# Two attention and two MLP layers on one core: the last 64 contraction rows of the projections as half-array pairs, with some reordering

## The chip, the core and the metric

The kernel runs on one core of one Trainium2 chip. The core has TensorE (PE: matrix multiplication into the accumulator memory, PSUM), VectorE (DVE), ScalarE (ACT), GpSimd (POOL) and SyncE (SP), which here issues the DMA transfers. Each engine works through its own instructions in order; the engines wait for each other by semaphores. The metric is the device time of one execution in microseconds (us), lower is better; the time before is the median of three runs.

## The reference

`x` has 2048 tokens of width 576. Four layers follow each other, A, B, A, B, each on the layer norm of `x` and added to it. The two A layers share their weights, and so do the two B layers.

```python
def _A_ref(x, wqkv, wo):
    B, S, D = x.shape
    H = 32; Dh = D // H                      # 18
    qkv = (x @ wqkv).reshape(B, S, 3, H, Dh).transpose(2, 0, 3, 1, 4)
    q, k, v = qkv[0], qkv[1], qkv[2]
    phi = lambda t: jnp.where(t > 0, t + 1, jnp.exp(t)) + 1e-6
    pq, pk = phi(q), phi(k)
    kv = jnp.einsum("bhsd,bhse->bhde", pk, v)
    z = jnp.einsum("bhsd->bhd", pk)
    num = jnp.einsum("bhqd,bhde->bhqe", pq, kv)
    den = jnp.einsum("bhqd,bhd->bhq", pq, z)[..., None] + 1e-6
    o = num / den
    return o.transpose(0, 2, 1, 3).reshape(B, S, D) @ wo

def _B_ref(x, w1, b1, w2, b2):               # D = 576, F = 4608
    y = _layernorm(x, axis=-1)
    h = _gelu(jnp.einsum("bsd,df->bsf", y, w1) + b1)
    return jnp.einsum("bsf,fd->bsd", h, w2) + b2

x = x + _A_ref(_layernorm(x), wqkv, wo)
x = x + _B_ref(_layernorm(x), w1, b1, w2, b2)
x = x + _A_ref(_layernorm(x), wqkv, wo)
x = x + _B_ref(_layernorm(x), w1, b1, w2, b2)
```

## The kernel before

The tokens are cut into 16 tiles of 128 (`NT`). The width 576 is the contraction of the projections; it is cut into five chunks (`KD`), four of 128 rows and one of 64. `yT` holds the normalised tokens transposed, chunk by chunk. In the fifth chunk only 64 of the 128 rows carry data in an A layer; the other 64 rows of the weights `wqkv_sb` are set to zero (L188), so the fifth matmul of every group runs on the full array with half of it at zero.

**Normalisation** (`LNPipe`, L234 to L350). `feed` enters a tile, each `tick` moves every entered tile one stage on: statistics on DVE (L266, L267, L272, L275), the root on POOL (L284), the normalisation on DVE (L303) or POOL (L288, L299), and the transposition into `yT`: by TensorE and a copy for the first six tiles of layer 0 (L324 to L332), by a DMA for all others (L343). In B layers POOL also copies the last 64 columns a second time beside themselves (L307), so that both halves of the fifth chunk carry them.

**Layer A** (`layer_A`, L399). A loop runs over the 16 tiles. In each, `k_proj` makes the keys in two halves of 288 columns, five matmuls each, in two buffers of the pool `ps_h` (four banks), followed by phi (`phi_from_psum`: two ACT passes, L361 and L363, and two DVE passes, L364 and L368). `v_proj` makes the values in two parts of 252 and 324 columns, five matmuls each, in the one buffer `accB` of the pool `ps_acc`; ACT copies 504 columns out (L438) and DVE the last 72 (L447). `kv_acc` of the tile before adds keys times values to `kvacc` (in `accA`), and from tile 4 on one block of `q_proj` (a group of heads `g`, a chunk of 512 tokens `c`) makes the queries, five matmuls of 512 columns. TensorE's order is exactly the order of the code (`pe` chains the instructions). In layer 0 `pre_a1` also feeds later tiles' normalisation; in layer 2 nearly all of that is done before.

After the loop come the masks of `kvacc` (L485), its product with `wo` (`kv_wo`, in `accB` and `accA` in turn, copied out by DVE or ACT, L512 and L514), the denominators (`den_stage`, `scale_stage`), the eight query blocks that are left, and the output stage: for each of 16 tiles `wo_stage` makes ten matmuls and `residual` adds the old rows on DVE into a buffer `xn` (L390, four buffers), which is stored and, for the first four tiles, normalised by POOL.

**Layer B** (`LayerB`). The first product of the MLP already runs as half-array pairs (L648): two matmuls of 64 contraction rows at once, one on each half of the array, in different PSUM banks. The second product (L695) uses the full array.

**Order.** Each engine's order is set when the program is built: a scheduler keeps the dependencies that `add_manual_dep` adds (`NOSYNC` ones only fix an order on an engine) and otherwise places instructions by readiness. SP's start-up DMAs follow the chain of `chained`: the first two token tiles, the keys' weights, a token tile, the values' weights, three token tiles, the queries' weights, the rest.

Of the kernel before, what the change touches and what calls it, by code (L numbers as in the profile page):

```python
# [17 lines left out]
KD = 5  # L18
# [16 lines left out]
def build(tc, A_x, A_wqkv, A_wo, B_w1, B_b1, B_w2, B_b2, out, dbg=None, n_layers=4):  # L35
    nc = tc.nc
    dbg = dbg or {}
    with ExitStack() as ctx:
# [71 lines left out]
        NV = 3  # L110
# [18 lines left out]
        x0_tiles = {}  # L129

# [30 lines left out]
        def load_wqkv(part):  # L161
            cols = slice(part * D, (part + 1) * D)
            chained(nc.sync.dma_start(out=wqkv_sb[:, 0:4, cols],
                                      in_=A_wqkv[0:4 * P, cols].rearrange("(k p) n -> p k n", p=P)))
            chained(nc.sync.dma_start(out=wqkv_sb[0:64, 4, cols], in_=A_wqkv[4 * P:D, cols]))
# [22 lines left out]
        nc.vector.memset(wqkv_sb[64:P, 4, :], 0.0)  # L188
        for vr in v_ring:
            nc.gpsimd.memset(vr[:, 4, 72:126], 0.0)  # L190
            nc.gpsimd.memset(vr[:, :, 126:127], 1.0)
            nc.gpsimd.memset(vr[:, :, 127:128], 0.0)

# [40 lines left out]
        class LNPipe:  # L234
# [3 lines left out]
            def feed(self, xt, t, kind, norm_eng, evac_eng="dve", load_from=None, after=None):  # L238
# [3 lines left out]
                                       after=after, xbar=xbar))  # L242
# [4 lines left out]
            def tick(self, transposes=1):  # L247
                for it in list(self.items):
# [14 lines left out]
                    elif st == 0:  # L263
# [8 lines left out]
                        nc.vector.bn_aggr(out=mv[:], in_=stt[:])  # L272
# [18 lines left out]
                    elif st in (2, 3):  # L291
# [10 lines left out]
                        else:  # L302
                            norm = nc.vector.tensor_scalar(out=y[:, 0:D], in0=xt[:, 0:D], scalar1=it["mv"][:, 0:1],  # L303
                                                           scalar2=it["rstd"][:, 0:1], op0=ALU.subtract, op1=ALU.mult)
                            dve_last["norm"] = norm.ins.name
                        if it["kind"] == "B":
# [12 lines left out]
                    elif st == 4:  # L319
                        y = it["y"]  # L320
                        t = it["t"]
                        tp = ps_h.tile([P, 8, P], BF16, name="tp", tag="h")
                        for k in range(KD):
                            pe(nc.tensor.transpose(out=tp[:, k, :], in_=y[:, k * P:(k + 1) * P], identity=ident[:]))  # L324
                        if it["evac"] == "both":
                            part = nc.vector.tensor_copy(out=yT[:, 0:2, t * P:(t + 1) * P], in_=tp[:, 0:2, :])  # L326
                            dve_last["turn"] = part.ins.name
                            nc.scalar.copy(out=yT[:, 2:KD, t * P:(t + 1) * P], in_=tp[:, 2:KD, :])
# [30 lines left out]
        def phi_from_psum(ps_ap, out_ap, rows, n, after=None):  # L359
            e = work.tile([P, 512], BF16, name="phi_e", bufs=3)  # L360
            act_last["exp"] = nc.scalar.activation(out=e[0:rows, 0:n], in_=ps_ap, func=ACT.Exp).ins.name  # L361
            a = work.tile([P, 512], BF16, name="phi_a", bufs=2)
            nc.scalar.activation(out=a[0:rows, 0:n], in_=ps_ap, func=ACT.Identity, bias=C1, scale=1.0)  # L363
# [21 lines left out]
        def residual(li, t, halves):  # L385
            xo = xo_of.pop((li, t))
            last = (li == n_layers - 1)
            xn = work.tile([P, D], F32, name="xn", tag="xn", bufs=4)
# [10 lines left out]
        def layer_A(li, next_kind, pre_a1=None, mid_k0=None):  # L399
            kvacc = ps_acc.tile([P, 2, 512], F32, name="kvacc", tag="accA")  # L400
# [4 lines left out]
            def k_proj(t, mid=None):  # L405
                tok = slice(t * P, (t + 1) * P)
                pk = blk.tile([P, D], BF16, name="pk", tag="blk")
                for half in range(2):
                    kp = ps_h.tile([P, 512], F32, name="k_ps", tag="h")
                    for k in range(KD):  # L410
                        pe(nc.tensor.matmul(kp[:, 0:HALF], lhsT=yT[:, k, tok],  # L411
                                         rhs=wqkv_sb[:, k, D + half * HALF: D + (half + 1) * HALF],
                                         start=(k == 0), stop=(k == KD - 1)))
# [6 lines left out]
            def v_proj(t):  # L420
# [6 lines left out]
                else:  # L427
                    vp = ps_acc.tile([P, 2, 512], F32, name="v_ps", tag="accB")
                    vps = None
                    first, second = vp[:, 0, :], vp[:, 1, :]  # L430
                for k in range(KD):
                    pe(nc.tensor.matmul(first[:, 0:252], lhsT=yT[:, k, tok], rhs=wqkv_sb[:, k, 2 * D: 2 * D + 252],  # L432
                                     start=(k == 0), stop=(k == KD - 1)))
                for k in range(KD):
                    pe(nc.tensor.matmul(second[:, 0:324], lhsT=yT[:, k, tok], rhs=wqkv_sb[:, k, 2 * D + 252: 3 * D],  # L435
                                     start=(k == 0), stop=(k == KD - 1)))
                if vps is None:
                    nc.scalar.copy(out=va[:, 0:4, 0:126].rearrange("p (b g) c -> p b g c", b=2),  # L438
                                   in_=vp[:, :, 0:252].rearrange("p b (g c) -> p b g c", g=2))
# [18 lines left out]
            def q_proj(g, c):  # L458
                qp = ps_h.tile([P, 512], F32, name="q_ps", tag="h")
                for k in range(KD):  # L460
                    pe(nc.tensor.matmul(qp[0:GR[g], :], lhsT=wqkv_sb[:, k, GO[g]:GO[g] + GR[g]],  # L461
                                     rhs=yT[:, k, c * CA:(c + 1) * CA],
                                     start=(k == 0), stop=(k == KD - 1)))
                pq[(g, c)] = blk.tile([P, D], BF16, name="pq", tag="blk")
                phi_from_psum(qp[0:GR[g], :], pq[(g, c)][0:GR[g], 0:CA], GR[g], CA)
# [3 lines left out]
            for t in range(NT):  # L469
# [9 lines left out]
                if t >= 4:  # L479
                    q_proj(*q_left.pop(0))  # L480
# [340 lines left out]
```

## Time and profile before

| | us |
|---|---|
| median of the runs (772.94, 774.46, 774.32) | 774.32 |
| profiled execution | 772.56 |
| its span, first to last instruction | 770.8 |
| TensorE busy | 760.2 |
| ACT, DVE, POOL busy | 329.0, 243.8, 124.9 |

The granted TensorE clock is 0.999 of full speed. By stages of the span:

| stretch, us | what runs | TensorE | DVE | ACT | POOL |
|---|---|---|---|---|---|
| 0 to 20 | layer 0, start and tiles 0 to 3 | 15.66 | 14.04 | 9.39 | 7.78 |
| 20 to 66.7 | layer 0, rest of the loop over tiles | 46.70 | 34.92 | 35.42 | 29.30 |
| 66.7 to 107.4 | layer 0, output stage | 39.40 | 34.09 | 23.68 | 10.12 |
| 107.4 to 389.2 | layer 1 (B) | 281.80 | 64.67 | 98.81 | 37.58 |
| 389.2 to 444.6 | layer 2, loop over tiles | 55.40 | 28.47 | 40.80 | 0.55 |
| 444.6 to 485.3 | layer 2, output stage | 39.40 | 34.09 | 23.63 | 10.07 |
| 485.3 to 770.8 | layer 3 (B) | 281.85 | 33.49 | 97.32 | 29.56 |

How to read the lines: a timeline line has the start in us, the time taken, the engine, the line of the code, the operation, what it writes and reads, the shapes and, after x, how many like it are merged. A bracket gives the idle time before it on its engine and what ended it. A line of the view by stretches has the bounds, the length and then the busy time of TensorE, of its weight loads, of DVE, ACT and POOL, the clock and the DMA share and rate. Matmuls overlap: the next one starts before the last has left the array, so what counts is the distance from start to start, not the duration that is shown.

### The profile page before, as it was taken

How to read it: one execution, taken by the hardware profiler on the slowest of the kernel's cores; microseconds unless marked ns; L12 is line 12 of the kernel's file. 1: busy time of each engine (PE TensorE's matmuls, PEld its weight loads, DVE VectorE, ACT ScalarE, POOL GpSimd, SP SyncE). 2: the span in 40 equal slices, each digit the busy share in tenths (PEclk: the TensorE clock that was granted, in tenths of full speed). 3: DMA queues.
4: the chain of work that ended last, by engine and by line, in shares of the span. 5: the costliest groups of instructions: out<-in, count | busy, mean ns of one | idle time of the engine just before them, and what ended most of it. 6: DMA issues, size and time to landing. Idle time of an engine off the chain costs nothing.

```text
span 770.8 us, 15615 instructions
## 1 busy us (share of the span) xinstructions
PE 760.2 (99%) x6516; PEld 490.0 (64%) x6520; DVE 243.8 (32%) x678; ACT 329.0 (43%) x733; POOL 124.9 (16%) x208
## 2 busy tenths in 40 slices
PE   7999999999999999999999999999999999999998
PEld 4776654675477457646777766547745764674476
DVE  7776952125013402301244488353000000000000
ACT  4777546304610650263057784460065026205600
POOL 3680412013000301100100004221010010011000
PEclk9999999999999999999999999999999999999999
DMA  8799484025112502400310038775100110011000
GB/s 257 160 242 327 129 275 97 19 62 131 45 40 73 143 2 64 94 2 24 89 47 1 1 108 263 201 147 89 46 26 1 32 62 1 13 43 39 2 29 18
DMA packets 77904, 66.41 MB, mean 86 GB/s; under 512 B 44682, under 2 KB 62474, under 8 KB 77834
## 3 DMA queue, kind: packets, MB, share of 16 engines
q1 hardware_dynamic: 77834, 65.42, 31.7%
q8 instruction: 51, 0.84, 0.5%
q14 instruction: 19, 0.16, 0.1%
HBM read 39.38 MB, written 16.52 MB: 73 GB/s over the span
## 4 chain that ended last, share of the span: by engine, by line
PE 92%; DVE 4%; POOL 2%; ACT 1%; issue 1%; POOLq 0%; DVEq 0%
PE m_ps L695 37%; PE h_ps L648 20%; PE hp_ps L648 16%; PE k_ps L411 5%; PE q_ps L461 5%; PE wo_ps L549 3%; PE v_ps L435 3%; PE v_ps L432 2%; PE kvacc L455 1%; DVE xn L390 1%; POOL ln_rstd L284 1%; POOL ln_nmr L288 1%; POOL y_ring L299 1%; DVE pq L541 0%; ACT rden_bc L540 0%
## 5 line engine op out<-in xcount | busy, mean ns | idle before, releaser
L695 PE MATMUL m_ps<-w_sb,hT 128*128 128x288 bf16 x2304 | 283.6, 286 | 0.0
L695 PEld LDWEIGHTS <-hT 128*128 128x128 bf16 x2304 | 224.8, 98 | 59.8 <-issue 3.4
L648 PEld LDWEIGHTS <-w_sb 64*128 64x128 bf16 x2304 | 124.5, 94 | 136.2 <-issue 1.9
L648 PE MATMUL hp_ps<-yT,w_sb 64*128 64x512 bf16 x1152 | 178.0, 376 | 0.0
L390 DVE TENSOR_TENSOR xn<-m_ps,x_ring 128x576 f32<-128x576 f32 (+1 forms) x32 | 24.2, 757 | 411.6 <-PE m_ps L695 411.6
L648 PE MATMUL h_ps<-yT,w_sb 64*128 64x512 bf16 x1152 | 147.9, 376 | 0.0
L653 ACT COPY relay_sb<-relay_sb 128x1 f32<-128x1 f32 x144 | 28.5, 198 | 265.7 <-PE h_ps L648 222.2
L644 ACT ACTIVATE hT<-h_ps,b1T 128x512 bf16<-128x512 f32 x144 | 91.0, 683 | 43.3 <-PE h_ps L648 43.3
L284 POOL TENSOR_TENSOR ln_rstd<-ln_u,neg_half 128x1 f32<-128x1 f32 x64 | 36.8, 576 | 359.7 <-DVE ln_u L275 229.5
L644 ACT ACTIVATE hT<-hp_ps,b1T 128x512 bf16<-128x512 f32 x144 | 91.1, 692 | 0.0
L382 POOL TENSOR_TENSOR x_ring<-x_ring,b_bc 128x576 f32<-128x576 f32 x32 | 40.7, 1275 | 240.6 <-DMA x_ring<-x_d 237.9
L648 PE MATMUL h_ps<-yT,w_tail 64*128 64x512 bf16 x144 | 54.1, 376 | 0.0
L648 PE MATMUL hp_ps<-yT,w_tail 64*128 64x512 bf16 x144 | 54.1, 376 | 0.0
L461 PE MATMUL q_ps<-yT,wqkv_sb 128*126 128x512 bf16 (+1 forms) x200 | 50.0, 382 | 0.1
L549 PE MATMUL wo_ps<-kvwo,pq 126*128 126x288 bf16 (+1 forms) x320 | 43.9, 286 | 2.3 <-DVE kvwo L512 0.9
L411 PE MATMUL k_ps<-wqkv_sb,yT 128*128 128x288 bf16 x320 | 44.8, 286 | 0.3 <-DVE yT L326 0.2
L361 ACT ACTIVATE phi_e<-k_ps 128x288 bf16<-128x288 f32 x64 | 27.0, 422 | 36.0 <-PE k_ps L411 35.9
L549 PEld LDWEIGHTS <-pq 126*128 126x128 bf16 (+1 forms) x320 | 30.4, 97 | 15.4 <-issue 4.2
L411 PEld LDWEIGHTS <-yT 128*128 128x128 bf16 x320 | 30.6, 98 | 12.2 <-DVE yT L326 0.7
L648 PEld LDWEIGHTS <-w_tail 64*128 64x128 bf16 x288 | 27.1, 94 | 17.1
L364 DVE TENSOR_SCALAR phi_e<-phi_e 128x288 bf16<-128x288 bf16 (+2 forms) x104 | 27.4, 264 | 24.1 <-ACT phi_e L361 23.7
L361 ACT ACTIVATE phi_e<-q_ps 126x512 bf16<-126x512 f32 (+1 forms) x40 | 24.0, 600 | 21.5 <-PE q_ps L461 21.3
(95 smaller groups left out, 542.5 us busy)
## 6 DMA issues: line engine op xcount, KB each, us to landing
x_ring<-x_d SPq DMA_DIRECT2D x66, 288.0 KB, 3.1
x_d<-xn SPq DMA_DIRECT2D x48, 288.0 KB, 2.4
w_sb<-in_B_w_dram SPq DMA_DIRECT2D x6, 864.0 KB, 8.6
w_sb<-in_B_w_dram SPq DMA_DIRECT2D x9, 512.0 KB, 5.1
x<-in_A_x_dram SPq DMA_DIRECT2D x16, 144.0 KB, 3.4
x_ring<-in_A_x_dram SPq DMA_DIRECT2D x16, 144.0 KB, 3.1
out_dram<-xn SPq DMA_DIRECT2D x16, 144.0 KB, 1.7
wqkv_sb<-in_A_wqkv_dram SPq DMA_DIRECT2D x3, 576.0 KB, 5.8
```

The costliest lines, as they stand in the source:

```text
L284: nc.gpsimd.tensor_tensor(out=rstd[:], in0=it["u"][:], in1=neg_half[:], op=ALU.pow)
L361: act_last["exp"] = nc.scalar.activation(out=e[0:rows, 0:n], in_=ps_ap, func=ACT.Exp).ins.name
L364: low = nc.vector.tensor_scalar(out=e[0:rows, 0:n], in0=e[0:rows, 0:n], scalar1=1.0, scalar2=1e-6, op0=ALU.min, op1=ALU.add)
L382: nc.gpsimd.tensor_tensor(out=xo, in0=xo, in1=b2_bc[:], op=ALU.add)
L390: total = nc.vector.tensor_tensor(out=res.rearrange("p (h n) -> p h n", h=2), in0=halves, in1=xo.rearrange("p (h n) -> p h n", h=2), op=AL ...
L411: pe(nc.tensor.matmul(kp[:, 0:HALF], lhsT=yT[:, k, tok], rhs=wqkv_sb[:, k, D + half * HALF: D + (half + 1) * HALF], start=(k == 0), stop=( ...
L461: pe(nc.tensor.matmul(qp[0:GR[g], :], lhsT=wqkv_sb[:, k, GO[g]:GO[g] + GR[g]], rhs=yT[:, k, c * CA:(c + 1) * CA], start=(k == 0), stop=(k ...
L549: pe(nc.tensor.matmul(wp[:, half, 0:HALF], lhsT=pq[(g, c)][0:GR[g], j * P:(j + 1) * P], rhs=kvwo[g][0:GR[g], half * HALF:(half + 1) * HALF ...
L644: act_last["gelu"] = nc.scalar.activation(out=hT[f][:, 0:CB], in_=dst[n], func=ACT.Gelu_apprx_tanh, bias=b1T[:, f:f + 1], scale=1.0).ins.name
L648: mm = pe(nc.tensor.matmul(dst[n], lhsT=wt, rhs=mv, start=(seen[n] == 0), stop=(seen[n] == 8)))
L653: relay = nc.scalar.copy(out=relay_sb[:, 1:2], in_=relay_sb[:, 0:1])
L695: pe(nc.tensor.matmul(acc[:, half, 0:HALF], lhsT=hT[f][:, j * P:(j + 1) * P], rhs=w2_sb[:, f, half * HALF:(half + 1) * HALF], start=(f == ...
```

## The change

**Half-array pairs.** In tiles 4 to 15 of layer 0 and in all tiles of layer 2, a new function `tails` runs first in each tile. It does the fifth chunk of both key halves on the lower 64 rows of the array and that of both value parts on the upper 64, alternating: key half 0 and values 0, key half 1 and values 1. `k_proj` and `v_proj` then add the four full chunks to the same accumulators. The weights of keys now lie in rows 0 to 63 of the fifth chunk and those of values in rows 64 to 127, with zeros in the other half; the zeros serve the tiles that still use the full array.

**Queries.** In five pairs of neighbouring tiles, the first (`q_open`) does the four full chunks of one query block and leaves it open; the next tile (`q_pair`) ends it in its tails, beside the first step of its own query block on the other half, then runs that block's phi and, after the values, its own block's four full chunks. The queries' weights of the fifth chunk lie in the lower or the upper half by group, which takes three DMAs instead of one. The query blocks are done in another order.

**The copy of the last 64 columns** is now made in A layers too, by POOL (L307's copy), or by a second short DVE pass for tiles 0, 1 and 3 of layer 0.

**Reorderings and buffers.** The first tile's transposes go to two PSUM buffers, `tp` and `tq`, copied by DVE and ACT. The second tile's `bn_aggr` follows the first tile's normalisation. The third tile's statistics follow the second tile's normalisation instead of its copy, and the fourth tile's follow the first tile's phi instead of the second's. The values of tile 0 are copied after the keys' phi. One late query block has its phi put behind `kv_wo`'s copies on DVE and ACT (`late_phi`). `xn` has five buffers instead of four and `v_ring` two instead of three. In layer 2 `kvacc` and the values swap their PSUM buffers.

```diff
-        NV = 3
+        NV = 2
...
+            tail = A_wqkv[4 * P:D, cols]
+            if part == 1:
+                chained(nc.sync.dma_start(out=wqkv_sb[0:64, 4, cols], in_=tail))
+            elif part == 2:
+                chained(nc.sync.dma_start(out=wqkv_sb[64:P, 4, cols], in_=tail))
+            else:
+                for odd in range(2):
+                    chained(nc.sync.dma_start(out=q_tail(odd, odd), in_=tail[:, 0:504].rearrange(
+                        "k (a b n) -> k a b n", a=2, b=2)[:, :, odd, :]))
+                chained(nc.sync.dma_start(out=wqkv_sb[64:P, 4, 504:D], in_=tail[:, 504:D]))
+
+        def q_tail(hi, odd):
+            return wqkv_sb[64 * hi:64 * (hi + 1), 4, 0:504].rearrange("k (a b n) -> k a b n", a=2, b=2)[:, :, odd, :]
...
-        nc.vector.memset(wqkv_sb[64:P, 4, :], 0.0)
+        nc.vector.memset(wqkv_sb[64:P, 4, D:2 * D], 0.0)
+        nc.vector.memset(wqkv_sb[0:64, 4, 2 * D:3 * D], 0.0)
...
-                        if it["kind"] == "B":
+                        if it["norm"] == "dve" and it["load"] is None and it["t"] in x0_here:
+                            nc.vector.tensor_scalar(out=y[:, D:DPAD], in0=xt[:, 4 * P:D], scalar1=it["mv"][:, 0:1],
+                                                    scalar2=it["rstd"][:, 0:1], op0=ALU.subtract, op1=ALU.mult)
+                        else:
                             nc.gpsimd.tensor_copy(out=y[:, D:DPAD], in_=y[:, 4 * P:D])
...
-            xn = work.tile([P, D], F32, name="xn", tag="xn", bufs=4)
+            xn = work.tile([P, D], F32, name="xn", tag="xn", bufs=5)
...
+            tag_k, tag_v = ("accA", "accB") if li == 0 else ("accB", "accA")
+            first_tails = 4 if li == 0 else 0
...
+            def tails(t, pair, opened):
+                tok = slice(t * P, (t + 1) * P)
+                kps = [ps_h.tile([P, 512], F32, name="k_ps", tag="h") for _ in range(2)]
+                vp = ps_acc.tile([P, 2, 512], F32, name="v_ps", tag=tag_v)
+                low = [(kps[half][:, 0:HALF], yT[0:64, 4, tok],
+                        wqkv_sb[0:64, 4, D + half * HALF:D + (half + 1) * HALF], True) for half in range(2)]
+                high = [(vp[:, 0, 0:252], yT[64:P, 4, tok], wqkv_sb[64:P, 4, 2 * D:2 * D + 252], True),
+                        (vp[:, 1, 0:324], yT[64:P, 4, tok], wqkv_sb[64:P, 4, 2 * D + 252:3 * D], True)]
+                qp = None
+                if pair is not None:
+                    (g, c), (g1, c1, qp1) = pair, opened
+                    qp = ps_h.tile([P, 512], F32, name="q_ps", tag="h")
+                    low.append((qp[0:GR[g], :], wqkv_sb[0:64, 4, GO[g]:GO[g] + GR[g]],
+                                yT[0:64, 4, c * CA:(c + 1) * CA], True))
+                    high.append((qp1[0:GR[g1], :], wqkv_sb[64:P, 4, GO[g1]:GO[g1] + GR[g1]],
+                                 yT[64:P, 4, c1 * CA:(c1 + 1) * CA], False))
+                for two in zip(low, high):
+                    for dst, wt, mv, first in two:
+                        pe(nc.tensor.matmul(dst, lhsT=wt, rhs=mv, start=first, stop=not first))
+                if pair is not None:
+                    q_phi(g1, c1, qp1)
+                return kps, vp, qp
...
-            q_left = [(g, c) for c in range(NCA) for g in range(G)]
+            q_single = {4: (4, 0), 15: (4, 1)}
+            q_open = {5: (1, 0), 7: (3, 0), 9: (1, 1), 11: (3, 1), 13: (1, 2)}
+            q_pair = {6: (0, 0), 8: (2, 0), 10: (0, 1), 12: (2, 1), 14: (0, 2)}
+            q_left = [(2, 2), (3, 2), (4, 2)] + [(g, 3) for g in range(G)]
+            opened = None
             pe_chain["on"] = True
             for t in range(NT):
+                kps = vp = qp = None
+                if t >= first_tails:
+                    kps, vp, qp = tails(t, q_pair.get(t), opened)
                 if li > 0 or t > 1:
-                    k_proj(t)
+                    k_proj(t, kps=kps)
                 elif t == 0:
                     k_proj(0, mid=mid_k0)
+                    dve_last["phi0"] = dve_last["phi"]
                     k_proj(1)
                 pre_a1(t)
-                v_proj(t)
+                v_proj(t, vp)
                 if t >= 1:
                     kv_acc(t - 1)
-                if t >= 4:
-                    q_proj(*q_left.pop(0))
+                if t in q_single:
+                    q_proj(*q_single[t])
+                elif t in q_open:
+                    (g, c), qp = q_open[t], ps_h.tile([P, 512], F32, name="q_ps", tag="h")
+                    q_main(g, c, qp, range(KD - 1), ended=False)
+                    opened = (g, c, qp)
+                elif t in q_pair:
+                    g, c = q_pair[t]
+                    q_main(g, c, qp, range(KD - 1), begun=True)
+                    q_phi(g, c, qp)
...
             kv_wo(2)
-            q_proj(*q_left.pop(0))
+            late_phi = q_proj(*q_left.pop(0), defer=True)
             for g in range(3, G):
                 scale_stage(g, 0)
             kv_wo(3)
             kv_wo(4)
+            late_phi(after=dve_last["kvwo"], act_after=act_last["kvwo"])
             q_proj(*q_left.pop(0))
...
         lnp.tick()
-        feed0(1, after=dve_last["u"])
         lnp.tick()
         lnp.tick()
+        feed0(1, after=dve_last["u"], agg_after=dve_last["norm"])
         lnp.tick()
...
-            feed0(2, after=lambda: dve_last["turn"])
+            feed0(2, after=dve_last["norm"])
...
-                feed0(t + 3, after=dve_last["phi"])
+                feed0(t + 3, after=dve_last["phi0" if t == 0 else "phi"])
```

`q_main` is the loop of matmuls of `q_proj` over given chunks, `q_phi` its call of `phi_from_psum`.

## The prediction

> **What bounds the kernel now.** I read four views of the profile in this order: the chain that ended last, TensorE's timeline at the borders between its modes, the timeline of all engines around one value projection, and TensorE's gaps at the start and in the output stages.
>
> ```profile
> PE 92%; DVE 4%; POOL 2%; ACT 1%; issue 1%; POOLq 0%; DVEq 0%
> ...
> 20.00:66.70 46.70, 46.70 (x379) 35.25 (x377) 34.92 (x122) 35.42 (x87) 29.30 (x51) 1.00 0.96 229
> 66.70:107.40 40.70, 39.40 (x340) 25.94 (x340) 34.09 (x85) 23.68 (x44) 10.12 (x16) 1.00 0.71 222
> ...
> 389.20:444.60 55.40, 55.40 (x453) 42.40 (x451) 28.47 (x106) 40.80 (x103) 0.55 (x1) 1.00 0.05 15
> ```
>
> TensorE is 92% of the chain. In both projection loops (20 to 66.7 us and 389.2 to 444.6 us) it never idles at clock 1.00, so matmul time taken out there shortens the kernel one for one, and so does a wait put in lengthen it.
>
> ```profile
> 177.33 0.65 PE L695 MATMUL m_ps<-w_sb,hT 128*128 128x288 bf16 x4
> 177.91 1.04 PE L648 MATMUL h_ps<-yT,w_sb 64*128 64x512 bf16 x8
> ...
> 142.22 0.38 PE L648 MATMUL hp_ps<-yT,w_tail 64*128 64x512 bf16 x1
> 142.53 1.15 PE L695 MATMUL m_ps<-w_sb,hT 128*128 128x288 bf16 x8
> ```
>
> These are the borders between full-array and half-array matmuls. The last full one starts at 177.33 + 0.65 - 0.286 = 177.69; the next, by its pitch of 35.39/288 = 0.123, could start at 177.82 but starts at 177.91: 0.096 lost. Back: a half-array pair takes 0.216 (nine in 1.94), yet 142.22 to 142.53 is 0.31: 0.095 lost. The first step after a border is about 0.01 longer. A round trip costs 0.21.
>
> ```profile
> 396.80 0.42 PE L455 MATMUL kvacc<-pk,v_ring 128*128 128x126 bf16 x5
> 397.00 0.58 ACT L438 CAST v_ring<-v_ps 128x504 bf16<-128x504 f32 x1 [0.51 <-PE v_ps L435]
> ...
> 397.06 1.39 PE L411 MATMUL k_ps<-wqkv_sb,yT 128*128 128x288 bf16 x10
> 397.61 0.23 DVE L447 CAST v_ring<-v_ps 128x72 bf16<-128x72 f32 x1 [0.74 <-ACT v_ring L438]
> ```
>
> The value accumulator `v_ps` has one buffer. Its emptying is ACT's copy, then DVE's, done at 397.84, which is 1.04 after TensorE went on to kvacc (1.10 with 0.06 for the signal). Today the ten key matmuls (1.23) cover it.
>
> ```profile
> 7.15 0.48 ACT L328 COPY yT<-tp 128x384 bf16<-128x384 bf16 x1 [4.87 <-DVE yT L326]
> 16.66 0.45 PE L324 MATMUL tp<-ident,y_ring 128*128 128x128 bf16 x5 [1.32 <-DVE ln_u L275]
> 79.30 1.58 PE L549 MATMUL wo_ps<-kvwo,pq 126*128 126x288 bf16 x10 [0.43 <-DVE kvwo L512]
> 97.27 1.42 DVE L390 TENSOR_TENSOR xn<-wo_ps,x_ring 128x576 f32<-128x576 f32 x2 [1.01 <-POOL y_ring L299]
> 98.08 1.39 PE L549 MATMUL wo_ps<-kvwo,pq 126*128 126x288 bf16 x10 [0.42 <-DVE xn L390]
> ```
>
> These are the waits that the reorderings aim at: the first tile's copy and the fourth tile's transposes at the start; a `kvwo` copy queued behind a phi, and an `xn` buffer still read by POOL, in the output stage.
>
> **The pairs.** A tile's four tail matmuls cost 2 x 0.123 (keys) + 0.108 + 0.138 (values: five in 0.54, five in 0.69 in the chain) = 0.492. As two pairs they cost the longer of each: 0.123 + 0.138, plus 0.004 each for the second start: 0.269. The round trip takes 0.21 of the 0.223 saved, so 0.01 is left per tile, 0.3 for 28 tiles. Ten tiles also pair two query tails, 0.216 for two instead of each: 0.212 x 10 = 2.1. Sum -2.4. Both directions of the border are in the trace, and the borders of the denominator's narrow matmuls lose 0.09 to 0.10 as well, so the bounds are -1.9 and -3.0.
>
> On the saving, the Trainium skill ("TensorEngine Tiling (Array Packing)", Overview, Theoretical Speedup) has up to 2x for a contraction of 64 or less, and by it alone the sum would be 28 x 0.223 + 2.1 = 8.4 us saved. The same page (Tiling Modes, Key Properties) says that changing the mode drains the array; it gives no price, but it speaks against so short a visit, and the two borders above agree with it.
>
> **The wait that the order adds.** Tails now stand first, and their second matmul writes `v_ps`. Queued behind it are all of TensorE's work of the tile. What covers the emptying is no longer the keys but only kvacc (0.26), the border (0.10) and a query block, if the tile has one.
> Layer 2, tiles 0 to 3 have none. The emptying ends 1.10 after kvacc's start, the pair could start after 0.36: 0.74 each, and 0.86 after tile 0, which has no kvacc: 3.1 us. From tile 4 on at least four query matmuls add 0.86, and 0.36 + 0.86 = 1.22 covers the 1.10. But in the tiles with a query pair ACT is late: the opened block's phi can start 0.7 into the tile, and 2 x 0.49 for it and 4 x 0.30 for the keys end at 2.9; with 0.58 + 0.23 and signals the emptying ends at 3.78, against 3.77 for the next pair: 0.1 in all. Layer 2: +3.2.
> Layer 0 pairs from tile 4. Tile 3 has no query block: 0.74 at least; in the trace DVE's copy there is done at 22.70, behind two statistics, 1.54 after kvacc's start, which makes 1.2. I take 1.0. For tiles 5 to 11 the instruction order puts the statistics of tile t+4 (two starts 0.37 apart) between the keys' last maximum and DVE's value copy. In a tile with a query pair ACT's last key step ends at 3.0; maximum 0.28, statistics 0.74, copy 0.21 and signals make 4.3, where 3.77 is wanted: 0.55, or 0.85 if the maximum takes 0.66 as at 31.90 instead of 0.31. In the tiles between, that step ends at 2.44 and the copy at 3.73 against 3.55: 0.2, or 0.5. Three paired and four others at the middle: 3 x 0.65 + 4 x 0.3 = 3.1. Layer 0: +4.1, between 3.1 and 5.6.
>
> The slow maximum at 31.90 runs while POOL normalises (31.37 to 32.41). The skill's page "SBUF — State Buffer" (Who interferes with whom) says that a DVE instruction with two SBUF inputs contends with a POOL instruction that reads SBUF; it speaks against the POOL copy added to every A tile, which by the page could only lengthen such steps, and by the row it is 0.24 long.
>
> **The start.** The fourth tile's statistics no longer follow the second tile's phi, and ACT's first copy no longer waits for DVE's. But the keys' weights land at 7.10, so the first key matmul stays at 7.17 and only the 0.25 wait inside it goes. After that DVE takes tile 2's statistics (1.0) before tile 1's copy, which makes that about 0.2 later. ACT now takes half of tile 1's values before tile 0's. Adding the steps up to the fourth tile's normalisation gives 16.25 for the transposes instead of 16.66: -0.4, between +0.3 and -1.0.
>
> **Output stages, twice.** With `kvwo` ahead of the late phi (0.21 + 0.34 and the wait for ACT), TensorE's 0.59 at 79.30 goes, and two waits of 0.2 after it. But DVE is busy 9.6 of the next 10 us, so the next wait, for `xn` at 88.74, moves only by the DVE idle that is removed (0.16 + 0.19 and a little): 0.4. The fifth `xn` buffer takes the wait for POOL out, 0.58. So -1.0 each, -2.0 together. Bounds: -0.4 (only DVE's idle) and -1.6 (with its neighbours) each.
>
> **At nothing.** The POOL copies (0.24 x 32) lie under TensorE's stream: a transpose's landing leads its use by 3.3 to 3.9 us (tile 6: 25.64, used 29.50); without that lead each costs 0.3. The two more weight DMAs (0.5 of SP each) delay the tokens' loads by 1 us; tile 6's land at 13.56 and are read after 17. Two value buffers suffice: a buffer is read by kvacc a whole tile (2.7) before it is written again.
>
> **Sum.** Span 770.8 - 2.4 + 3.2 + 4.1 - 0.4 - 2.0 = 773.3, +2.5. The profiled execution took 772.56, 1.8 around its span, so 775.1; the three runs have a median of 774.32, and on that scale I predict **776.8 us**.
>
> **Rivals.**
> *Faster, about 772.* The output stages lose all their gaps (2.8 us each on TensorE, by adding up its starts), the start gives 0.8, and the value wait stays at its lower bound, 3.2 + 3.1: 6.3 - 2.4 - 0.8 - 5.6 = -2.5. It decides once the stages give over 2.4 each. The waits named on 79.30 and 98.08 speak for it; against it is DVE, 34.1 of 40.7 us busy in that stage. Chance 0.14.
> *No change, about 774.5.* Lower wait, 6.3, and stages at 1.5 each, start -0.8: 0.1. Chance 0.22.
> *Slower still, about 779.5.* POOL's extra copy catches DVE's maximum in most tiles: layer 0 at 5.6, stages at -0.4 each, start 0: +3.2 + 5.6 - 2.4 - 0.8 = +5.6. For it speaks DVE at 0.75 and POOL at 0.63 busy in that loop. Chance 0.18.
> *My forecast,* with its own range of 775.9 to 778.5: 0.46.
>
> Slower by over 0.2% (1.5 us, about what a measurement of this kernel can tell from no change) is the forecast and the last rival, 0.64; same 0.22; faster 0.14. The range 773.0 to 780.5 leaves out most of the faster case and the tail above.
>
> **What would show it.** In the new profile, the second tail matmul in layer 2's tiles 1 to 4 should follow the first by 0.7 or more, named on DVE's value copy; layer 0's paired tiles should last 4.3, the others about 3.75; from tile 12 on two tiles should take 7.3 to 7.4 instead of 7.63. The transposes near 16.66 should start near 16.25, the first output matmul should wait for no `kvwo`. I am wrong if the pairs' second matmul starts at once there (the emptying is faster than the row), if a round trip costs much more or less than 0.21, or if the output stages shrink by over 2 us each.

## The result, and the profile after

The changed kernel takes 779.11 us (median of 6 runs, 778.85 to 779.22); the kernel before, run beside it, takes 773.35. The ratio is 1.0073, with a 95% interval of 1.0060 to 1.0086: 5.8 us slower, where 776.8, that is 2.5 slower, had been predicted. The profiled spans are 777.5 and 770.8 us; the profile of before is of its fastest run, so the spans are further apart (6.7) than the medians.

In the chain that ended last the shares of before have hardly moved, although 6.7 us were lost: TensorE's waits are spread over many steps.

```profile
PE 92%; DVE 4%; ACT 2%; issue 1%; DMA 1%; SPq 0%; DVEq 0%
```

The stretches show where the time went. The borders are those of before, moved by what each had shifted. Columns: stretch, its length, then busy time and instruction count of PE, PEld, DVE, ACT and POOL, TensorE's granted clock, the DMA share and GB/s.

```profile
20.00:74.20 54.20, 47.38 (x374) 30.79 (x372) 38.54 (x122) 34.84 (x85) 29.46 (x62) 1.00 0.95 232
74.20:113.90 39.70, 39.09 (x343) 25.89 (x340) 34.06 (x85) 23.72 (x44) 9.70 (x16) 1.00 0.57 181
395.70:452.50 56.80, 54.89 (x452) 36.89 (x452) 28.59 (x106) 40.33 (x103) 0.80 (x2) 1.00 0.07 19
```

TensorE was never idle in either projection loop before. Now it idles 54.20 - 47.38 = 6.8 us in layer 0's loop and 1.9 us in layer 2's. The loops are 7.5 and 1.4 us longer, the output stage 1.0 shorter. One line of the view of waits (engine, line, releaser: total, times, longest) holds nearly all of that idle time (only time with no matmul in the array is counted, so it is less than the delays added up below):

```profile
PE v_ps L455 <- DVE v_ring L508: 8.0, 11, 1.4
```

The timeline of layer 2, between tile 1 and tile 2, shows one such wait by itself:

```profile
401.34 0.42 PE L516 MATMUL kvacc<-pk,v_ring 128*128 128x126 bf16 x5
...
401.54 0.58 ACT L497 CAST v_ring<-v_ps 128x504 bf16<-128x504 f32 x1 [0.15 <-PE v_ps L494]
...
401.69 0.29 PE L455 MATMUL k_ps<-wqkv_sb,yT 64*128 64x288 bf16 x1
402.15 0.23 DVE L508 CAST v_ring<-v_ps 128x72 bf16<-128x72 f32 x1 [0.39 <-ACT v_ring L497]
402.44 0.27 PE L455 MATMUL v_ps<-wqkv_sb,yT 64*128 64x252 bf16 x1 [0.45 <-DVE v_ring L508]
```

The first tail matmul of the new tile starts right behind the border, at 401.69. Its partner writes `v_ps`, which ACT and then DVE are still emptying, and starts at 402.44, 1.10 after kvacc: the number that the prediction had worked out from before.

Two places where the change gains: the fourth tile's transposes start at 15.98 instead of 16.66, and the first output matmul waits for nothing (no bracket behind it).

```profile
15.98 0.44 PE L349 MATMUL tp<-ident,y_ring 128*128 128x128 bf16 x5
...
86.21 1.44 PE L634 MATMUL wo_ps<-kvwo,pq 126*128 126x288 bf16 x10
```

Lining up both traces at the same matmuls, and adding up how much later than the first tail matmul its partner starts in each tile (without a wait they start together), gives this balance of the spans (us). The row of the pairs is not measured by itself: it is what the loops' shifts leave once the waits are taken off.

| term | predicted | measured |
|---|---|---|
| start | -0.4 | -0.5 |
| waits for `v_ps`, layer 0 | +4.1 | +9.5 |
| waits for `v_ps`, layer 2 | +3.2 | +3.1 |
| pairs, both loops | -2.4 | -3.3 (-1.5 and -1.8) |
| output stages | -2.0 | -2.1 |
| sum | +2.5 | +6.7 (spans: +6.7) |

The miss comes from one row. Layer 0's waits before tiles 4 to 13 are 1.14, 0.14, 0.57, 0.85, 0.41, 0.69, 0.96, 1.67, 1.50 and 1.60; three of them are about twice the 0.74 that the emptying costs in layer 2. The timeline around the one before tile 12, of 1.50:

```profile
55.58 0.66 DVE L398 TENSOR_TENSOR pk<-phi_a,phi_e 128x288 bf16<-128x288 bf16 x1
...
56.03 0.63 POOL L71 MEMSET head_bc<- 128x640 bf16 x1
...
56.17 0.58 DVE L394 TENSOR_SCALAR phi_e<-phi_e 128x288 bf16<-128x288 bf16 x1
56.27 0.58 ACT L497 CAST v_ring<-v_ps 128x504 bf16<-128x504 f32 x1
...
56.80 0.97 POOL L67 TENSOR_SCALAR_AFFINE_SELECT head_bc<-head_bc 128x630 bf16<-128x630 bf16 x1
56.85 1.04 DVE L398 TENSOR_TENSOR pk<-phi_a,phi_e 128x288 bf16<-128x288 bf16 x1
...
57.82 0.45 DVE L283 BATCH_NORM_STATS2 ln_st<-x 128x6 f32<-128x288 bf16 x1
58.19 0.43 DVE L284 BATCH_NORM_STATS2 ln_st<-x 128x6 f32<-128x288 bf16 x1
...
58.55 0.21 DVE L508 CAST v_ring<-v_ps 128x72 bf16<-128x72 f32 x1
...
58.81 0.26 PE L455 MATMUL v_ps<-wqkv_sb,yT 64*128 64x252 bf16 x1 [1.21 <-DVE v_ring L508]
```

ACT's copy ended at 56.85; DVE's 0.21 copy started 1.7 later. Ahead of it in DVE's queue stood a phi step of 0.58 (0.24 in layer 2), a maximum of 1.04 (0.31 in layer 2; a maximum, like the phi step before it, is part of the keys' phi) and two statistics. The two slow steps run beside POOL's fill of a mask and its select.

### The profile page after: what moved, and what is told of

Its sections match the earlier page's. It is cut to its first block, busy times and chain, and to the rows that moved or that the text cites. A ratio compares the mean times of both kernels' runs of the same rounds, so it can differ in the third digit from the quotient of the medians.

```text
span 777.5 us, 15644 instructions
## 1 busy us (share of the span) xinstructions
PE 760.7 (98%) x6520; PEld 480.6 (62%) x6520; DVE 249.2 (32%) x685; ACT 328.5 (42%) x733; POOL 128.4 (17%) x234
## 4 chain that ended last, share of the span: by engine, by line
PE 92%; DVE 4%; ACT 2%; issue 1%; DMA 1%; SPq 0%; DVEq 0%
PE m_ps L780 36%; PE h_ps L733 20%; PE hp_ps L733 16%; PE wo_ps L634 5%; PE q_ps L521 4%; PE k_ps L467 4%; PE v_ps L494 2%; PE v_ps L491 1%; DVE pk L398 1%; PE rden_ps L623 1%; PE v_ps L455 1%; DVE phi_e L394 1%; PE kvacc L516 1%; ACT phi_e L387 1%; DMA x<-in_A_x_dram 1%
## 5 line engine op out<-in xcount | busy, mean ns | idle before, releaser
L521 PE MATMUL q_ps<-yT,wqkv_sb 128*126 128x512 bf16 (+1 forms) x180 | 45.7, 383 | 0.1
L394 DVE TENSOR_SCALAR phi_e<-phi_e 128x288 bf16<-128x288 bf16 (+2 forms) x104 | 30.2, 292 | 32.7 <-ACT phi_e L387 32.4
L467 PE MATMUL k_ps<-wqkv_sb,yT 128*128 128x288 bf16 x264 | 38.0, 287 | 0.9 <-DVE yT L358 0.6
L467 PEld LDWEIGHTS <-yT 128*128 128x128 bf16 x264 | 23.2, 98 | 13.8 <-issue 7.8
```

Source lines behind the costliest of these rows:

```text
L394: low = nc.vector.tensor_scalar(out=e[0:rows, 0:n], in0=e[0:rows, 0:n], scalar1=1.0, scalar2=1e-6, op0=ALU.min, op1=ALU.add)
L467: pe(nc.tensor.matmul(kp[:, 0:HALF], lhsT=yT[:, k, tok], rhs=wqkv_sb[:, k, D + half * HALF: D + (half + 1) * HALF], start=(k == 0 and not ...
```

## The experiments

The theory: the lost time is the emptying of the one `v_ps` buffer, which the keys used to cover, made longer in layer 0 by DVE's queue. The rivals: the switches of the array, POOL's added copy, the reorderings. The expectations count a wait beyond the 0.12 at which one matmul of 288 columns follows another, so 0.12 less for each: 8.3 in all for layer 0, with 1.54, 1.38 and 1.48 before tiles 11 to 13, and 2.6 for layer 2. The measured waits of the runs are given in the same way. Each run is compared with the kernel before on the same chip (medians 773.58, 772.88 and 772.95 for the first four, next four and last four runs); between runs of different groups, and with the changed kernel's 779.11, a difference of some 0.7 us tells nothing.

**1. Pairs behind the keys.** The same pairs and switches; the eight full key matmuls come first, and `k_proj` no longer makes them.

```
 def tails(t, pair, opened):
+    for half in range(2):
+        for k in range(KD - 1):
+            pe(nc.tensor.matmul(kps[half][:, 0:HALF], lhsT=yT[:, k, tok], rhs=..., start=(k == 0), stop=False))
...
-    low = [(kps[half][:, 0:HALF], ..., True) for half in range(2)]
+    low = [(kps[half][:, 0:HALF], ..., False) for half in range(2)]
```

> The same pairs, but after the tile's eight full key matmuls instead of ahead of them. Theory (the emptying of v_ps is no longer covered): the key matmuls add 0.98 us of cover, so all of layer 2's waits (2.6) and nearly all of layer 0's (8.3; its longest, 1.54, keeps some 0.5) go: 779.1 - 10.4 = 768.7, between 767.5 and 770, below both kernels, and the first pair starts without a wait. Rival 1 (the pairs with their two switches of the array per tile are what costs): their number is unchanged, so 778.5 to 780. Rival 2 (the key phis, which now end later, turn into a new wait on the k_ps buffers): 771 to 775 with that wait named on k_ps.

Measured: 771.60 us, ratio 0.9980 (0.9971 to 0.9989). The pairs and switches are all there and the time is 7.5 below the changed kernel's, so the first rival falls. It is above the 767.5 to 770 expected. Layer 2 has no wait left. Layer 0 keeps three waits for `v_ps`, 0.65, 1.55 and 1.48 beyond the pitch, more than the 0.5 expected, and one of 1.33 before the bias transpose, which needs a buffer that a late phi still reads: a wait of the second rival's kind, though not on `k_ps`. In the view of waits:

```profile
PE v_ps L460 <- DVE v_ring L512: 3.2, 3, 1.4
...
PE tp L240 <- ACT phi_a L392: 1.2, 1, 1.2
```

Even 0.98 more cover doesn't hide DVE's copy in the late tiles: before the wait of 1.55 it starts 1.7 after ACT's has ended (50.64 and 52.35).

**2. Reorderings and buffers alone.** No pairs; the query blocks in the order of before.

```
-    first_tails = 4 if li == 0 else 0
+    first_tails = NT
...
+    q_left = [(g, c) for c in range(NCA) for g in range(G)]
+    q_single = {t: q_left.pop(0) for t in range(4, NT)}
+    q_open, q_pair = {}, {}
```

> The reorderings and buffers alone: no tail pairs, the query blocks in the order of before. Theory: start -0.7 and output stages -1.05 and -1.08 stay, nothing else: 773.35 - 2.8 = 770.5, between 769.8 and 771.3; no wait on v_ps. Rival (the reorderings or the POOL copy in every tile slow the loop of layer 0): 773 or more, with tiles 5 to 13 of layer 0 longer than in before.

Measured: 772.11 us, ratio 0.9983 (0.9975 to 0.9992), a gain of 1.5 instead of 2.8. The start (-0.8 at the accumulation of tile 2) and both output stages (-1.1 each) are as expected, and nothing waits for `v_ps`. But two waits are new, for the transposed tokens `yT`:

```profile
56.81 1.40 PE L467 MATMUL k_ps<-wqkv_sb,yT 128*128 128x288 bf16 x10 [0.93 <-DMA yT<-y_ring]
...
62.00 0.42 PE L467 MATMUL k_ps<-wqkv_sb,yT 128*128 128x288 bf16 x2 [1.22 <-DMA yT<-y_ring]
```

That has nothing to do with pairs. In before the transpose of tile 14 is issued at 53.44 and lands 6.3 later, at 59.74, for a matmul at 60.03: a lead of 0.3 us only. Here it is issued at 54.49 and lands 7.5 later.

**3. Pairs only from tile 5 on.** `first_tails = 5` in both layers.

> Both layers make pairs only from tile 5 on, so every pair stands behind a tile with a query block. Theory: layer 2 loses its four waits (0.73 and 3 x 0.62 = 2.6), layer 0 the one before tile 4 (1.0), the rest of layer 0's 7.2 stays: 779.1 - 3.6 = 775.5, between 774.9 and 776.2. Rival (the wait only moves to the first tile that has pairs): 778 to 779.

Measured: 775.21 us, ratio 1.0022 (1.0014 to 1.0031). Layer 2 has no wait, layer 0 none before tile 5 or earlier; the wait doesn't move on to the next tile.

**4. ACT empties `v_ps` alone.** In tiles with pairs ACT also copies the last 72 columns.

```
-    if t == 0:
+    if t == 0 or t >= first_tails:
         nc.scalar.copy(out=va[:, 4, 0:72], in_=second[:, 252:324])
     else:
         nc.vector.tensor_copy(out=va[:, 4, 0:72], in_=second[:, 252:324])
```

> In the tiles with pairs ACT copies the last 72 value columns too, right after its 504, so DVE and what stands ahead in its queue no longer end the emptying. Theory (in layer 0 the emptying is late because DVE is: statistics and phi steps stretched beside POOL's work): layer 0's waits fall from 8.3 to 3 to 4, layer 2's stay within 0.3 of 2.6: 779.1 - 4.8 = 774.3, between 773.3 and 776. Rival (the two copies themselves, or ACT's late phis, set it): within 1 of 779.1.

Measured: 772.40 us, ratio 0.9986 (0.9977 to 0.9995), 6.7 below the changed kernel and below the 773.3 expected at the least. In layer 0 only the first `v_ps` wait (1.02, before tile 4) is left, in layer 2 0.73 and 3 x 0.47. So layer 0's waits were DVE's lateness, not the copies' own time. The view of waits shows what came in their place, 1.19 and 1.33 beyond the pitch before tiles 12 and 14:

```profile
PE k_ps L455 <- DMA yT<-y_ring: 2.2, 2, 1.2
...
PE v_ps L455 <- ACT v_ring L506: 1.5, 4, 0.6
```

The next three runs go after these tokens.

**5. Run 2 without POOL's copy.** The run leaves out the last 64 contraction rows of the values and of half the queries, so only its time counts.

```
-    else:
+    elif it["kind"] == "B":
         nc.gpsimd.tensor_copy(out=y[:, D:DPAD], in_=y[:, 4 * P:D])
```

> The run without pairs (772.1 us), and in layers 0 and 2 POOL doesn't copy the last 64 columns: there the value and half of the query tails take old rows, so these 64 contraction rows are left out of them. Theory (the copy, which POOL does behind mask steps and SP's transpose behind it, makes the tokens of tiles 13 and 14 late): the two waits on yT, 1.09 and 1.38 beyond the matmuls' pitch, go, and their transposes are issued about 1 us earlier: 772.1 - 2.3 = 769.8, between 769.2 and 770.6. Rival (the tokens are late because the loop starts 0.7 earlier, while the weights' transfers hold the queues as before): 771.5 to 772.5, with the waits still there.

Measured: 772.18 us, ratio 0.9988 (0.9977 to 0.9999), but from 770.85 to 774.36 in 12 runs. The execution profiled took 770.85, the fastest, and has one wait for `yT`, 0.63 beyond the pitch; the others were not profiled. The median did not move: the theory of this run falls.

**6. Run 2 with masks and weight pieces ordered behind POOL's copy.**

```
-    tc.add_manual_dep(step().ins, pool_last["norm"], NOSYNC, ...)
+    tc.add_manual_dep(step().ins, pool_last["copy"], NOSYNC, ...)
...
-    gate["dep"] = pool_last["norm"]
+    gate["dep"] = pool_last["copy"]
```

> The run without pairs (772.1 us), with the masks and the MLP's weight pieces ordered behind POOL's copy instead of behind its normalisation; nothing is left out. Theory (not the copy's 0.23 itself, but what is let in ahead of it on POOL and ahead of the transpose on SP): both waits on yT go or fall below 0.3 in all: 770.0, between 769.3 and 770.8. Rival 1 (the copy's own 0.23 to 0.35): about 771.3, the waits smaller by a third at most. Rival 2 (the weights' transfers): 772 with the waits unchanged.

Measured: 772.85 us, ratio 1.0003 (0.9988 to 1.0018), from 771.36 to 776.66. The profiled execution took 775.12; tile 14's transpose was issued at 56.16 and landed 7.0 later:

```profile
63.24 1.03 PE L467 MATMUL k_ps<-wqkv_sb,yT 128*128 128x288 bf16 x7 [2.95 <-DMA yT<-y_ring]
```

Order on POOL does not mend it. Rival 2, the weights' transfers, is what remains.

**7. All mended but the transfers.** Edits 1, 4 and 6 together, the bias transpose at tile 5.

> Pairs behind the key matmuls, ACT empties v_ps alone in tiles with pairs, masks and weight pieces behind POOL's copy, the bias transpose at tile 5 instead of 8. Theory: nothing of the change's price is left and all its gains are: 773.4 - 0.7 (start) - 2.1 (output stages) - 2.4 (pairs) = 768.2, between 767.5 and 769.2; waits on v_ps below 0.5 in all. Rival (the tokens, wanted 1.2 us earlier still by tile 15, become layer 0's bound): 769.3 to 771 with waits on yT in tiles 12 to 15.

Measured: 771.24 us, ratio 0.9980 (0.9967 to 0.9993), from 769.78 to 775.17. No wait for `v_ps` is left; three for `yT` are, 1.31, 0.50 and 1.53 before tiles 10, 12 and 14. The rival was right in kind; it had put the waits into tiles 12 to 15 and the time at 771 at most.

**8. Large masks early.** In the changed kernel, `mask_steps = mask_steps[11:] + mask_steps[:11]`.

> The changed kernel with the order of the mask steps turned round: the large ones (quad_mask, head_bc) stand in tiles 4 to 7, the small ones after. Theory (DVE's phi steps are stretched beside POOL's large mask steps, and the copy that empties v_ps stands behind them): the waits before tiles 11, 12 and 13 (1.54, 1.38, 1.48) fall to 0.5 to 0.9 each and those before tiles 5 to 8 (0, 0.45, 0.72, 0.28) rise to 0.5 to 1.4 each; the sum stays near 8.3 and the time within 1.5 of 779.1. Rival (something else that belongs to the late tiles): the waits stay where they are within 0.3 each.

Measured: 779.02 us, ratio 1.0076 (1.0063 to 1.0089). The waits before tiles 11, 12 and 13 fell to 0.73, 0.28 and 0.10, those before tiles 6 and 7 rose from 0.45 to 0.68 and from 0.72 to 2.26: they went where the large masks went. Those before tiles 5 and 8 did not rise (0.01 and 0.04); in tile 7, ahead of the latter, TensorE ran at half clock. The time did not fall with the sum of the waits (6.1 instead of 8.3), for a reason told at the end. The timeline ahead of tile 7:

```profile
33.48 1.00 DVE L396 TENSOR_SCALAR phi_e<-phi_e 128x288 bf16<-128x288 bf16 x1
...
34.52 0.96 POOL L67 TENSOR_SCALAR_AFFINE_SELECT head_bc<-head_bc 128x630 bf16<-128x630 bf16 x1
34.58 1.03 DVE L400 TENSOR_TENSOR pk<-phi_a,phi_e 128x288 bf16<-128x288 bf16 x1
...
36.82 0.22 DVE L510 CAST v_ring<-v_ps 128x72 bf16<-128x72 f32 x1
...
37.09 0.27 PE L457 MATMUL v_ps<-wqkv_sb,yT 64*128 64x252 bf16 x1 [2.09 <-DVE v_ring L510]
```

A key maximum is again stretched to 1.03 beside a select of the same mask, five tiles earlier.

**9. Run 7 with nine weight pieces moved to the end of the loop (two) and behind it (seven).**

```
-    for _ in range(2 if t in (4, 7, 10) else 1):
+    for _ in range(2 if t == NT - 1 else 1 if t < 10 else 0):
         late_pieces.pop(0)()
...
     prefetch_xo(li, t, add_b2=False)
+while late_pieces:
+    late_pieces.pop(0)()
 kv_wo(0)
```

> The run with everything mended (771.2 us), with nine of the MLP's 17 weight pieces taken out of layer 0's loop: one piece per tile from tile 2 to 9, none from 10 to 14, two at tile 15, seven behind the output stage's first rows. Theory (what is left of the loss, 1.3 + 0.5 + 1.5 in three waits on yT, is tokens whose transposes share the queues with weight pieces): these waits go: 768.2, between 767.4 and 769.0, and the runs lie within 1 us of one another. Rival (the pieces moved make the output stage's rows or the MLP's first w2 late): 769.5 to 772, with a wait of TensorE or DVE on x_ring or w_sb.

Measured: 766.73 us (766.63 to 766.97), ratio 0.9918 (0.9904 to 0.9931): 6.2 us faster than before, 12.4 faster than the changed kernel, and the best of all; the expectation, 767.4 at the least, was too slow. Its chain of waits, and then its stretches:

```profile
PE 97%; DVE 1%; DMA 1%; ACT 0%; issue 0%; SPq 0%; DVEq 0%
```

```profile
20.00:64.80 44.80, 44.80 (x372) 30.04 (x371) 34.12 (x110) 34.52 (x96) 30.42 (x62) 1.00 0.70 153
64.80:104.40 39.60, 39.08 (x343) 25.88 (x343) 34.14 (x86) 24.13 (x46) 9.62 (x16) 1.00 1.04 326
```

TensorE has no idle time in layer 0's loop, where the DMA share is 0.70 instead of 0.95; it is 1.04 in the output stage, with no wait for rows. The transposes of tiles 13 to 15 now land 2.6 after their issue.

**10. Run 2 with the weight pieces moved in the same way.**

> The run without pairs (772.1 us) with the weight pieces moved in the same way; POOL's order is as in the changed kernel. Theory (the weights' transfers make the tokens of tiles 13 and 14 late, POOL's copy only lengthens the way to them): 773.1 - 0.7 - 2.1 = 770.3, between 769.6 and 771.0, no wait on yT over 0.3, runs within 1 us. Rival (POOL's copy behind the masks is enough to make them late): 771.3 to 772.5 with waits on yT at tiles 13 and 14.

Measured: 770.07 us (769.87 to 770.24), ratio 0.9960 (0.9948 to 0.9973). No wait for `yT`. Runs 2 and 10 differ by the pieces alone, 2.0 us: the transfers held the tokens up, with POOL's copy where it was.

**11 and 12. The changed kernel with the pieces moved, with and without the statistics behind the value copy.** Run 12 has the edit of run 9 to the pieces alone; run 11 has this too:

```
+    dve_last["v"] = nc.vector.tensor_copy(out=va[:, 4, 0:72], in_=second[:, 252:324]).ins.name
...
-    pre_a1(t)
+    if li > 0 or t < 4:
+        pre_a1(t)
     v_proj(t, vp)
+    if li == 0 and t >= 4:
+        pre_a1(t)
...
-    feed0(t + 4, after=dve_last["phi"])
+    feed0(t + 4, after=dve_last["v" if t >= 4 else "phi"])
```

> The changed kernel with the weight pieces moved, and from tile 4 of layer 0 on the statistics of the later tile ordered behind DVE's value copy instead of ahead of it. Theory (two causes add up: statistics of 0.74 ahead of the copy in tiles 5 to 11, and phi steps stretched beside POOL): the waits before tiles 6 to 12 lose up to 0.74 each (0.45, 0.72, 0.28, 0.56, 0.74, 0.74, 0.74), 4.2 in all, and the one before tile 13 stays near 1.5: 4.2 below the run without this edit, 774.9, between 774 and 776. Rival (the stretched steps alone): within 1.5 of the run without this edit.

> The changed kernel with the weight pieces moved alone, the base of the run with the statistics behind. Theory (in the changed kernel no wait is on tokens): 779.1, within 0.7, waits on v_ps as before within 0.3 each. Rival (the weights' transfers take part in stretching DVE's steps or in delaying the tokens' statistics): 776 to 778.

Measured: run 12 778.84 us, ratio 1.0077 (1.0064 to 1.0091), each wait within 0.01 of the changed kernel's; so transfers have no part in its loss. Run 11 772.16 us, ratio 0.9987 (0.9978 to 0.9996): 6.7 lower, where 4.2 was expected. Of layer 0's waits 1.02 (before tile 4), 0.52 (before tile 14, where the changed kernel has none) and 0.12 (before tile 7) are left. More went than the 0.74 of two statistics per tile, and the wait of 1.48 before tile 13 went too, which had been expected to stay. The changed kernel's timeline ahead of tile 13 has no statistics in DVE's queue at all:

```profile
61.60 0.64 ACT L497 CAST v_ring<-v_ps 128x504 bf16<-128x504 f32 x1
61.72 1.03 POOL L67 TENSOR_SCALAR_AFFINE_SELECT head_bc<-head_bc 128x630 bf16<-128x630 bf16 x1
61.84 1.00 DVE L394 TENSOR_SCALAR phi_e<-phi_e 128x288 bf16<-128x288 bf16 x1
...
62.88 2.00 POOL L67 TENSOR_SCALAR_AFFINE_SELECT head_bc<-head_bc 128x630 bf16<-128x630 bf16 x2
62.95 1.03 DVE L398 TENSOR_TENSOR pk<-phi_a,phi_e 128x288 bf16<-128x288 bf16 x1
...
63.90 0.22 DVE L508 CAST v_ring<-v_ps 128x72 bf16<-128x72 f32 x1
...
64.17 0.26 PE L455 MATMUL v_ps<-wqkv_sb,yT 64*128 64x252 bf16 x1 [1.30 <-DVE v_ring L508]
```

So two stretched steps alone can make a long wait. (An estimate from these rows: at 0.23 and 0.31 the two would be done before ACT's copy, at 62.24, and DVE's 0.22 would end before the first tail matmul, at 62.58.) Run 11 took them away as well: in its trace the key maxima ahead of the value copies of tiles 10 to 12 take 0.66 beside POOL's normalisation, and the selects run beside other DVE steps (a query's maximum takes 1.06, 0.43 otherwise). Where one stretched key step is left ahead of a copy, a phi step of 0.99 in tile 13, stands the wait of 0.52. Run 11 thus moves both causes, and what the statistics cost by themselves was not measured.

## Why the prediction was right, and where it was wrong

*The added wait* was the right mechanism, and where DVE has nothing else to do the size was right too: in layer 2 the partner is 0.86 late after tile 0 and 0.74 after each of the next three, as worked out; only the 0.1 for the paired tiles there did not come. The time itself lies outside the forecast's own range, 775.9 to 778.5, and inside only the wide one, which was to take in "Slower still" as well. That rival's reason did not come, so the hit is in part luck.

*Layer 0 is the step that failed*: "Layer 0: +4.1, between 3.1 and 5.6", out of "Three paired and four others at the middle". Its middle values, 0.65 and 0.3, also lie 0.05 below the middles of their own bounds (0.55 and 0.85, 0.2 and 0.5), 0.35 in all. Counted by the tile whose values are emptied, that is one before the tile that waits: for tile 3 the sum had 1.0, measured 1.14; for tiles 5 to 8 0.3, 0.65, 0.3, 0.65, measured 0.57, 0.85, 0.41, 0.69. For tiles 9 to 12 it had 0.3, 0.65, 0.3 and nothing, measured 0.96, 1.67, 1.50 and 1.60: 5.7 instead of 1.25, 4.5 of the 5.4 that are missing. The upper bound took one row, the maximum of 0.66 at 31.90, as the worst case of a DVE step beside POOL. Maxima of 0.73 to 1.04 and phi steps of 0.58 to 1.00 stand beside the large masks, which the instruction order puts into just these tiles. Before had the same masks, but there the selects ran beside other steps: no key maximum took more than 0.66 and no key phi step more than 0.69, and the key matmuls covered the emptying. Tile 12 counted as free because it has no statistics of its own. Run 8 moved the waits with the masks, run 4 took them away with DVE, run 11 by an order that moved statistics and masks.

*The pairs* give 3.3 by what is left over (predicted 2.4, at most 3.0), and 0.09 to 0.10 each way at the borders is as predicted. Two tiles with one query pair and no wait take 7.35 instead of 7.63 (layer 2, 416.56 to 423.91). In run 9, which has 0.5 of waits, the two loops are 2.8 shorter than before; by the medians runs 9 and 10 differ by 3.3.

*Output stages* give 1.05 and 1.08 (predicted 1.0 each), the *start* 0.5 to 0.7 (0.4). The start is the weakest of these numbers: in the profiles of the twelve runs, which have the same start, the fourth tile's transposes begin at 15.57 to 16.59.

*At nothing* was wrong in its reason. "A transpose's landing leads its use by 3.3 to 3.9 us" was read at tile 6. At tile 14 the lead is 0.3, because the weights' transfers lengthen the way from 2.7 to 6.3. In the changed kernel it cost nothing, as run 12 shows, only since the waits for `v_ps` delay the use as well. Without those waits it costs 2.0 (runs 2 and 10).

*The rivals.* "Slower still" had named its place rightly (POOL beside DVE's maximum in layer 0), at 779.5 (its sum, +5.6, gives 779.9), but put it down to POOL's extra copy, and had the gains fail with it. The trace speaks against the copy: two key maxima that overlap it, at 28.61 and 46.05, take 0.31 as elsewhere. The changed kernel was not run without it. The faster case needed output stages at over 2.4 each, and they gave 1.1; a faster kernel came only with the wait mended and the weight pieces moved (766.7 in run 9).

## What to carry to other kernels

When work is moved in front of a wait, price the wait from the row of every tile it will meet, not from one: the emptying's last engine had 0.2 of work there, and 0 to 1.7 us in its queue ahead of it, by what POOL did at that moment. A buffer's slack is a lead that shrinks along a loop, so read it at the last tile. And put short array-mode visits where something else covers the buffer they write: with the weight pieces moved, the pairs at the head of the tile cost 8.8 us over the kernel without pairs (runs 12 and 10), and behind the keys, with the rest mended, they are part of one 3.3 us faster than it (run 9).

## What was not expected of the hardware

A TensorE idle time of about 2 us cost more than itself. In run 8, behind the 2.09 us of idle time before 37.09, the granted clock (third column from the right) fell to half:

```profile
37.10:37.90 0.80, 0.80 (x7) 0.49 (x7) 0.59 (x4) 0.00 (x0) 0.40 (x1) 0.94 1.09 345
37.90:41.20 3.30, 3.30 (x17) 2.15 (x16) 2.52 (x5) 1.47 (x5) 3.09 (x6) 0.50 1.11 260
```

For 3.3 us each matmul of 288 columns took 0.24 instead of 0.12, some 1.6 us more: that takes up most of the 2.2 us by which run 8's waits are shorter. In run 6, behind 2.95 us, the clock was 0.56 from 64.0 to 67.5. Behind idle times of 1.37 us (run 7, and the changed kernel's waits) it stayed at 1.00. So here a wait that grew beyond about 2 us nearly doubled its price. Runs 6 and 7 scatter over 5.3 and 5.4 us, where run 9 scatters over 0.3, and all their executions above 774 and 771 us have a mean granted clock of 0.998 or less, the faster ones 0.999 or more. Run 5 scatters over 3.5 us with the clock at 0.998 to 1.000, so the clock alone doesn't make the scatter; that the waits for tokens differ from execution to execution would, but wasn't looked at. The Trainium skill ("TensorE: Matmul & The Clock Gate", section "What's actually happening") gives an idle window of about 3.4 us before the clock falls to half; here 2.1 us were enough.

DVE's steps beside POOL were stretched from 0.31 up to 1.04 (maximum, two inputs) and from 0.23 up to 1.00 (phi step, one input). The stretched steps ahead of tiles 12 and 13 that run beside a select end about 0.1 after it: 57.89 and 57.77, 62.84 and 62.75. The skill ("SBUF — State Buffer", section "Who interferes with whom") has DVE and POOL exclude each other for such forms, and the rows agree; what it costs was only to be had by looking at which POOL instruction stands beside.
